# A batch-by-batch attention and bilinear FFN kernel: early batches one K chunk per head pair, first k and v over two fp32 queues, outputs at each strip's end, late loads behind the transposes of q

## The chip, the cores and the metric

The kernel runs on one core of a Trainium2 chip. Its metric is the device time of one execution in microseconds (us); lower is better. A core has TensorE (PE, matrix products into PSUM), VectorE (DVE), ScalarE (ACT), GpSimd (POOL) and SyncE (SP). Each engine takes its instructions in program order. Transfers are issued by SP, ACT or POOL; here POOL issues all that convert fp32 to bf16 on the way.

## The reference

```python
def _attn_ref(q, k, v, g_norm):            # q, k, v: 8 batches, 8 heads, 576 tokens, 64
    kv = np.einsum('bhsd,bhse->bhde', k, v)
    out = np.einsum('bhsd,bhde->bhse', q, kv)
    rms = np.sqrt(np.mean(out * out, axis=-1, keepdims=True) + 1e-06)
    return out / rms * g_norm
...
    x = attn_out.transpose(0, 2, 1, 3).reshape(B * S, H * D)      # 4608 tokens, 512
...
    a = x @ w_a                                                   # 512 to 1536
    b = x @ w_b
    return (a * b) @ w_out                                        # 1536 to 512
```

All inputs and the output are fp32. There is no softmax: for each head the kernel forms the 64x64 product of k and v, and multiplies q by it.

## The kernel before, in words

The work on TensorE is in bf16. The normalised x is kept transposed in four tiles `xt[0..3]`, 128 of the 512 model columns each (a "K chunk"), 4608 tokens long. The FFN goes over 9 strips of 512 tokens. For each strip there are 12 "units" (`Unit`, `ffn_ab`), one for each 128 of the 1536 inner columns: four matmuls with w_a, four with w_b (L205), a copy of the first product by ScalarE (L219) and a product by VectorE into `abt` (L221). Then come four output groups (`ffn_o`, `o_mm` L249, `o_out`), each 12 matmuls of 512 columns for 128 tokens, a copy to `o_sb` by VectorE and ScalarE in turn (L264, L262), and a store from SP (`store`, L242).

Attention goes batch by batch; batch b has 576 tokens, so strip s needs batches up to s, and strip s + 1 needs batch s + 1. For a batch: `kv` (L131) multiplies k by v for each pair of heads, `kv_out` (L140) copies that to bf16, `x` (L164, L171) multiplies q by it and squares the result, and `ss` (L176, L179, L184) sums the squares over a head with a matmul, takes the reciprocal root on ScalarE, and writes `xt` on VectorE.

q must be there transposed (`qT`, two tiles in turn). Batches 0 and 1 (`EARLY`) load q with tokens on partitions and transpose on TensorE (`qtr`, L147). For batches 2 to 7, `load_late` loads k and v, and copies q to a DRAM tile `qs` in bf16; then `transpose_q` (L118) has SP issue one transposing transfer from qs to qT. k and v have three buffers (`NB`), so load_late(b) waits for kv of batch b - 3.

Heads p and p + 4 make a pair, so that one x group of two pairs fills chunks m and m + 2; the chunks are used in the order `KORD`.

The program's order is written out by hand. POOL's queue: the pairs of batch 0, w_a and w_b in pieces of 256 columns (`load_ab`), w_out in 12 pieces (`load_o`), the pairs of batch 1, then `load_late` of batches 2 to 7. TensorE: dummy matmuls on zeros between the pieces of batch 0 (L310 to L328), strip 0's units, strip 0's outputs interleaved with batch 1 (L341 to L367), and then from strip 1 on a loop (L395) that sets pieces of the batch b = s + 1 between the units (`slices`), and the outputs of the strip before behind every third unit. transpose_q and load_late of the batch after the next are issued behind unit 6 of a strip. PSUM has 8 banks: units rotate through banks 0 to 2, outputs have bank 3 (`O`), x has banks 4 and 5 (early also 0 and 1), the sums 6 and 7, kv a part of 6 or 7.

Of the kernel before, what the change touches and what calls it, by code (L numbers as in the profile page):

```python
# [15 lines left out]
def kernel(  # L16
# [23 lines left out]
    EPS = 1e-6  # L40

    EC, EP = 6, 96
    EARLY = 2

    KORD = (0, 2, 1, 3)

    pool = ctx.enter_context(tc.tile_pool(name="sb", bufs=1))
    psum = ctx.enter_context(tc.tile_pool(name="ps", bufs=1, space=bass.MemoryType.PSUM))
# [26 lines left out]
    zeros = sb([128, 128], BF16, "zeros")  # L75
    g_col = sb([128, 1], FP32, "g_col")
    eps_t = sb([128, 1], FP32, "eps_t")
    warm = sb([128, 1], FP32, "warm")
    xv = [xt_i for xt_i in xt]

    P = psum.tile([128, 8, STRIP], FP32, name="P", tag="P")
    O = 3
# [6 lines left out]
    def load_heads(b, t, src, hs):  # L89
        nc.gpsimd.dma_start(  # L90
            out=t[:, hs, :, :], in_=src[b, hs].rearrange("h (t c) d -> t h c d", c=EC)
        )

    def load_pair(b, p):
        hs = slice(p, H, NP)
        load_heads(b, kt[b % NB], k, hs)
        load_heads(b, vt[b % NB], v, hs)
        load_heads(b, qt[b], q, hs)
# [6 lines left out]
        nc.gpsimd.dma_start(out=wo_t[:, i, :], in_=wo_v[:, i, :])  # L105

    def load_late(b):
        load_heads(b, kt[b % NB], k, slice(0, H))
        load_heads(b, vt[b % NB], v, slice(0, H))
        d = qs_d[b].rearrange("t (p j d) -> t p j d", p=NP, j=2)  # L110
        for j in range(2):
            nc.gpsimd.dma_start(  # L112
                out=d[:, :, j, :],
                in_=q[b, j * NP : (j + 1) * NP].rearrange("h t d -> t h d"),
            )

    def transpose_q(b):
        nc.sync.dma_start_transpose(qT[b % 2], qs_d[b])  # L118


    class Attn:
        def __init__(self, b):
            self.b = b
            self.kvs = kvs[b % 2]
            self.qT = qT[b % 2]

        def kv(self, p, o):

            for c in range(EC):
                for j in range(2):  # L130
                    nc.tensor.matmul(  # L131
                        o[j * D : (j + 1) * D, :],
                        lhsT=kt[self.b % NB][:, p + j * NP, c, :],
                        rhs=vt[self.b % NB][:, p + j * NP, c, :],
                        start=(c == 0),
                        stop=(c == EC - 1),
                    )
# [4 lines left out]
        def qtr(self, p, i0, i1):
            for h, i in ((0, i0), (1, i1)):
                t = P[:, i, :].bitcast(BF16)[:, 0:HF].rearrange("q (c t) -> q c t", c=EC // 2)
                for c in range(EC // 2):
                    for j in range(2):
                        nc.tensor.transpose(  # L147
                            t[j * D : (j + 1) * D, c, :],
                            qt[self.b][:, p + j * NP, h * (EC // 2) + c, :],
                            ident[0:EP, 0:EP],  # L150
                        )
                dst = self.qT[:, p, h * HF : (h + 1) * HF]
                src = P[:, i, :].bitcast(BF16)[:, 0:HF]
                if h:
                    nc.scalar.copy(dst, src)
                else:
                    nc.vector.tensor_copy(dst, src)
# [36 lines left out]
    class Unit:  # L194
# [15 lines left out]
                    stop=(kc == KORD[-1]),  # L210
                )

        def first(self):
            self.mm(wa_t, KORD[:2])
            self.mm(wb_t, KORD[:2])

        def rest(self, kcs=KORD):
            self.mm(wa_t, kcs)
# [64 lines left out]
    make_identity(nc, ident)  # L283
# [26 lines left out]
    dummy(30, 0)  # L310
    kv1(A, 0)
    A.qtr(0, 2, 3)
    dummy(4, 0)
    kv1(A, 1)
    A.qtr(1, 2, 3)
    dummy(6, 0)
    A.x(0, 0, X0)
    A.x(0, 1, X1)
    kv1(A, 2)
    A.qtr(2, 2, 3)  # L320
    A.ss(0, 0, SS, X0)
    dummy(4, 2)
    A.ss(0, 1, SS, X1)
    kv1(A, 3)
    A.qtr(3, 2, 3)
    dummy(6, 2)
    A.x(1, 0, X0)
    A.x(1, 1, X1)  # L328
    u0 = Unit(0, 0, 2, 3)
    u1 = Unit(0, 1, 0, 1)  # L330
    u0.first()
    A.ss(1, 0, SS, X0)
    A.ss(1, 1, SS, X1)
    u0.rest(KORD[2:])
    u1.rest()
    n_ab[0] = 2
# [8 lines left out]
    A.qtr(0, 2, 1)
    o_mm(0, 1, O, h1)
    kv1(A, 1)
    A.qtr(1, 2, 1)
# [3 lines left out]
    A.qtr(2, 2, 1)
    A.x(0, 0, X0)
    o_mm(0, 2, O, h1)
    A.x(0, 1, X1)
    A.ss(0, 0, SS, X0)
# [15 lines left out]
    u0.first()
    A.ss(1, 1, SS, X1)
    u0.rest(KORD[2:])
    u1.rest()
    n_ab[0] = 2


    def slices(A, per):
        kb = P[:, 7, 0 : NP * D].rearrange("q (p e) -> q p e", e=D)  # L380
        for p in range(NP):
            A.kv(p, kb[:, p, :])
            if p % per == per - 1:
                if p == NP - 1:
                    A.kv_out(0, NP, kb)
                yield
        for i, (m, h) in enumerate(((0, 0), (1, 0), (0, 1), (1, 1))):
            A.x(m, h, X0)
            yield
            A.ss(m, h, SS, X0)  # L390
            yield
            if i < 3:
                yield

    for s in range(1, N_STRIP):  # L395
        b = s + 1
        gen = slices(Attn(b), 4 if s == 1 else 2) if b < B else iter(())
        for fc in range(FC):
            if s > 1 or fc > 1:
                ffn_ab(s, fc)  # L400
            if s > 1 or fc > 0:
                next(gen, None)
            if fc % 3 == 2 and s > 1:
                ffn_o(s - 1, fc // 3)
                next(gen, None)
            if fc == 6 and b + 1 < B:
                transpose_q(b + 1)
                if b + 2 < B:
                    load_late(b + 2)
        for _ in gen:  # L410
            pass
# [41 lines left out]
```

## Time and profile before

| | |
|---|---|
| median of 3 runs | 357.5 us (356.81 to 357.6) |
| the profiled execution: its time | 358.61 us |
| its span, first to last instruction | 356.8 us |
| mean granted TensorE clock | 0.955 |
| busy, TensorE / VectorE / ScalarE / POOL | 324.0 / 120.2 / 125.8 / 59.9 us |
| moved by transfers | 32.19 MB |

The profile is of one execution. Matmuls are pipelined, so that a row of four matmuls of 512 columns lasts 1.03 us though the next group can start before its end; the distance of starts is what a group costs. The granted clock is 1.00 at 2.4 GHz and 0.50 at 1.2 GHz. In the waits a line names who waited, for whose result, and how long.

### The profile page before, as it was taken

To read this page: it belongs to the slowest core of one execution; us is meant where nothing else is said; L and a number is where in the kernel's file an instruction comes from. 1 tells how busy PE (TensorE), PEld (TensorE's weight loads), DVE (VectorE), ACT (ScalarE), POOL (GpSimd) and SP (SyncE) were. 2 spreads that over 40 slices of the span, in tenths; PEclk is the share of its full clock that TensorE was granted. 3 is DMA by queue.
4 is the path that set the end of the run, shared out by engine and by line. 5 is a ranking of instruction groups with operands and counts; after the bars stand their busy time and mean duration, and the time that the engine had idled before them with its cause. 6 is when DMAs were issued, how large, how long until landed. Compare 5 with 4: busy or idle time off the path is not lost.

```text
span 356.8 us, 4969 instructions
## 1 busy us (share of the span) xinstructions
PE 324.0 (91%) x1996; PEld 152.0 (43%) x2030; DVE 120.2 (34%) x204; ACT 125.8 (35%) x214; POOL 59.9 (17%) x78
## 2 busy tenths in 40 slices
PE   5779998706979999999999999999999999999996
PEld 4524443302434444444444444444444444444443
DVE  0323422301452543344434434352435232332311
ACT  2433334402453444344334433542453312223201
POOL 8845985230005000500000000000000000000000
PEclk9569999975999999999999999999999999999999
DMA  7999999999913940694100400130001000010022
GB/s 97 188 196 201 199 211 209 194 148 148 177 14 46 184 96 29 99 160 113 43 26 20 112 31 29 48 79 31 29 31 29 30 32 29 29 59 32 29 59 90
DMA packets 70024, 32.19 MB, mean 90 GB/s; under 512 B 43760, under 2 KB 65520, under 8 KB 70000
## 3 DMA queue, kind: packets, MB, share of 16 engines
q0 software_dynamic: 50304, 18.88, 46.4%
q1 hardware_dynamic: 19696, 12.98, 14.4%
q8 instruction: 16, 0.26, 0.3%
q14 instruction: 8, 0.07, 0.1%
HBM read 37.75 MB, written 12.98 MB: 142 GB/s over the span
## 4 chain that ended last, share of the span: by engine, by line
PE 68%; issue 0%; ACT 0%; ACTq 0%
PE P L205 41%; PE P L249 23%; PE P L131 1%; PE P L164 1%; PE P L176 1%; ACT osb L262 0%; ACT osb L421 0%; ACTq L421 0%
## 5 line engine op out<-in xcount | busy, mean ns | idle before, releaser
L221 DVE TENSOR_TENSOR ab<-P,asb 128x512 bf16<-128x512 f32 x108 | 74.7, 692 | 154.0 <-PE P L205 150.2
L205 PE MATMUL P<-xt,wa_t 128*128 128x512 bf16 x422 | 113.9, 387 | 5.2 <-DVE xt L184 4.1
L205 PE MATMUL P<-xt,wb_t 128*128 128x512 bf16 x424 | 113.0, 385 | 0.5
L249 PE MATMUL P<-wo_t,ab 128*128 128x512 bf16 (+1 forms) x428 | 97.4, 373 | 1.6 <-ACT osb L262 0.7
L219 ACT CAST asb<-P 128x512 bf16<-128x512 f32 x108 | 63.3, 586 | 93.6 <-PE P L205 93.1
L205 PEld LDWEIGHTS <-wb_t 128*128 128x128 bf16 x432 | 42.9, 99 | 53.4 <-issue 4.2
L249 PEld LDWEIGHTS <-ab 128*128 128x128 bf16 x444 | 42.7, 98 | 48.7 <-issue 1.1
L205 PEld LDWEIGHTS <-wa_t 128*128 128x128 bf16 x432 | 40.4, 99 | 48.9 <-issue 7.5
L184 DVE SCALAR_TENSOR_TENSOR xt<-P,g_col,rs 128x288 bf16<-128x288 f32 x64 | 30.1, 513 | 23.5 <-ACT rs L179 23.5
L171 ACT ACTIVATE sq<-P 128x576 bf16<-128x576 f32 x32 | 20.6, 652 | 41.6 <-PE P L164 41.6
L179 ACT ACTIVATE rs<-P,eps_t 128x576 f32<-128x576 f32 x32 | 23.7, 741 | 25.7 <-PE P L176 25.7
L264 DVE COPY osb<-P 128x512 f32<-128x512 f32 x18 | 12.4, 691 | 38.9 <-PE P L249 33.7
L262 ACT COPY osb<-P 128x512 f32<-128x512 f32 x17 | 10.0, 586 | 41.9 <-PE P L249 27.9
L90 POOL DMA_DIRECT2D kt<-in_k_dram x14 | 11.0, 786 | 75.9 <-PE P L131 70.2
L164 PE MATMUL P<-qT,kvs 64*64 64x288 bf16 x128 | 10.4, 328 | 12.1 <-DMA qT<-qs 12.1
L112 POOL DMA_DIRECT2D qs<-in_q_dram x12 | 20.5, 2018 | 4.2 <-DMA qs<-in_q_dram 3.1
L176 PE MATMUL P<-sq,ones 128*128 128x288 bf16 x64 | 14.1, 305 | 2.6 <-ACT rs L179 1.6
L131 PE MATMUL P<-vt,kt 96*64 96x64 bf16 x384 | 10.1, 202 | 5.2 <-DMA vt<-in_v_dram 3.5
L164 PEld LDWEIGHTS <-kvs 64*64 64x64 bf16 x128 | 3.6, 108 | 23.9 <-issue 21.3
L131 PEld LDWEIGHTS <-kt 96*64 96x64 bf16 x384 | 8.3, 116 | 12.4 <-issue 11.4
L176 PEld LDWEIGHTS <-ones 128*128 128x128 bf16 x64 | 6.4, 103 | 10.5 <-issue 4.4
L90 POOL DMA_DIRECT2D vt<-in_v_dram x14 | 10.8, 768 | 0.2
(26 smaller groups left out, 52.5 us busy)
## 6 DMA issues: line engine op xcount, KB each, us to landing
out_dram<-osb SPq DMA_DIRECT2D x23, 256.0 KB, 2.0
kt<-in_k_dram POOLq DMA_DIRECT2D x6, 576.0 KB, 11.1
vt<-in_v_dram POOLq DMA_DIRECT2D x6, 576.0 KB, 13.8
qs<-in_q_dram POOLq DMA_DIRECT2D x12, 288.0 KB, 15.3
out_dram<-osb SPq DMA_DIRECT2D x14, 128.0 KB, 2.3
wa_t<-in_moe_w_a_dram POOLq DMA_DIRECT2D x6, 256.0 KB, 10.0
wb_t<-in_moe_w_b_dram POOLq DMA_DIRECT2D x6, 256.0 KB, 10.3
wo_t<-in_moe_w_out_dram POOLq DMA_DIRECT2D x12, 128.0 KB, 5.9
```

The costliest lines, as they stand in the source:

```text
L90: nc.gpsimd.dma_start(out=t[:, hs, :, :], in_=src[b, hs].rearrange("h (t c) d -> t h c d", c=EC))
L112: nc.gpsimd.dma_start(out=d[:, :, j, :], in_=q[b, j * NP : (j + 1) * NP].rearrange("h t d -> t h d"),)
L131: nc.tensor.matmul(o[j * D : (j + 1) * D, :], lhsT=kt[self.b % NB][:, p + j * NP, c, :], rhs=vt[self.b % NB][:, p + j * NP, c, :], start=( ...
L164: nc.tensor.matmul(P[c * D : (c + 1) * D, i0 + j, 0:HF], lhsT=self.kvs[r, 2 * m + c, :], rhs=self.qT[r, 2 * m + c, ts], start=True, stop=True,
L171: nc.scalar.activation(sq[(2 * m + h) % 3], P[:, i0 : i0 + 2, 0:HF], AF.Square)
L176: nc.tensor.matmul(P[:, i0 + j, 0:HF], lhsT=ones, rhs=sq[n][:, j, :], start=True, stop=True)
L179: nc.scalar.activation(rs[n], P[:, i0 : i0 + 2, 0:HF], AF.Abs_reciprocal_sqrt, bias=eps_t)
L184: nc.vector.scalar_tensor_tensor(out=xt[m + 2 * j][:, t0 : t0 + HF], in0=P[:, x0 + j, 0:HF], scalar=g_col, in1=rs[n][:, j, :], op0=ALU.mul ...
L205: nc.tensor.matmul(self.a if w is wa_t else self.b, lhsT=w[:, kc, self.fc * 128 : (self.fc + 1) * 128], rhs=xt[kc][:, t0 : t0 + STRIP], st ...
L219: nc.scalar.copy(self.t, self.a)
L221: nc.vector.tensor_mul(abt[self.s % 2][self.fc], self.b, self.t)
L249: nc.tensor.matmul(P[:, i, e0:e1], lhsT=abt[s % 2][fc][:, g * 128 : (g + 1) * 128], rhs=wo_t[:, fc, e0:e1], start=(fc == 0), stop=(fc == F ...
```

## The change

- Batches 0 and 1 take heads 2p and 2p + 1 as a pair (`load_pair`, `head`), so that pair p gives chunk p of x. `x` and `ss` are replaced for them by `px`, `psq`, `pss`, `pst`, one pair at a time; `qtr` transposes a whole pair into one bank, and VectorE alone copies it. `KORD` is 0, 1, 2, 3.
- k and v of batch 0's first pair come as fp32, k from SP and v from ScalarE's queue, and are cast by VectorE and ScalarE. POOL makes the identity before its first load.
- The dummy matmuls have 512 columns: 8 ahead, and 2 + 4 for each of the pairs 0 to 2.
- The first 256 columns of w_a and w_b come in two pieces each, by K chunks.
- Batch 1 is spread more finely between the outputs of strip 0.
- load_late has q before k and v. For b above 2 it begins with a copy of one element on POOL, which reads the qT tile that transpose_q(b - 1) writes.
- From strip 1 on a strip's four outputs follow its own 12 units, with two banks in turn; the pieces of the batch stand at fixed places (`slot`). transpose_q(3) and load_late(4) come behind strip 1; transpose_q(b + 1) and load_late(b + 2) behind unit 8 of the strips from 2 on. The last strip stands by itself.

```diff
-    KORD = (0, 2, 1, 3)
+    KORD = tuple(range(KC))
...
     def load_pair(b, p):
-        hs = slice(p, H, NP)
+        hs = slice(2 * p, 2 * p + 2)
...
     def load_late(b):
-        load_heads(b, kt[b % NB], k, slice(0, H))
-        load_heads(b, vt[b % NB], v, slice(0, H))
+        if b > EARLY:
+
+            nc.gpsimd.tensor_copy(gate, qT[(b - 1) % 2][0:1, 0, 0:1])
         d = qs_d[b].rearrange("t (p j d) -> t p j d", p=NP, j=2)
...
+        load_heads(b, kt[b % NB], k, slice(0, H))
+        load_heads(b, vt[b % NB], v, slice(0, H))
...
+        def qtr(self, p, i, parts=1):
+            t = P[:, i, :].bitcast(BF16)[:, 0:S].rearrange("q (c t) -> q c t", c=EC)
+            for c in range(EC):
+                for j in range(2):
+                    nc.tensor.transpose(
+                        t[j * D : (j + 1) * D, c, :],
+                        qt[self.b][:, self.head(p, j), c, :],
+                        ident[0:EP, 0:EP],
+                    )
+            n = S // parts
+            for i0 in range(0, S, n):
+                nc.vector.tensor_copy(
+                    self.qT[:, p, i0 : i0 + n], P[:, i, :].bitcast(BF16)[:, i0 : i0 + n]
+                )
+
+
+        def px(self, p, i0):
+            for h in range(2):
+                for j in range(2):
+                    r = slice(j * D, (j + 1) * D)
+                    nc.tensor.matmul(
+                        P[r, i0 + h, 0:HF],
+                        lhsT=self.kvs[r, p, :],
+                        rhs=self.qT[r, p, h * HF : (h + 1) * HF],
+                        start=True,
+                        stop=True,
+                    )
+
+        def psq(self, p, i0):
+            nc.scalar.activation(sq[p % 3], P[:, i0 : i0 + 2, 0:HF], AF.Square)
+
+        def pss(self, p, i0, hs=(0, 1)):
+            for h in hs:
+                nc.tensor.matmul(
+                    P[:, i0 + h, 0:HF], lhsT=ones, rhs=sq[p % 3][:, h, :], start=True, stop=True
+                )
+            h0, h1 = hs[0], hs[-1] + 1
+            nc.scalar.activation(
+                rs[p % 3][:, h0:h1, :],
+                P[:, i0 + h0 : i0 + h1, 0:HF],
+                AF.Abs_reciprocal_sqrt,
+                bias=eps_t,
+            )
+
+        def pst(self, p, x0, hs=(0, 1)):
+            for h in hs:
+                t0 = self.b * S + h * HF
+                nc.vector.scalar_tensor_tensor(
+                    out=xt[p][:, t0 : t0 + HF],
+                    in0=P[:, x0 + h, 0:HF],
+                    scalar=g_col,
+                    in1=rs[p % 3][:, h, :],
+                    op0=ALU.mult,
+                    op1=ALU.mult,
+                )
...
     g_src = g_norm.rearrange("(d u) -> d u", u=1)
+    make_identity(nc, ident)
+    nc.sync.dma_start(out=k32, in_=pair_src(k, 0))
+    nc.scalar.dma_start(out=v32, in_=pair_src(v, 0))
     nc.vector.memset(zeros, 0.0)
-    load_pair(0, 0)
+    load_heads(0, qt[0], q, slice(0, 2))
...
-    for i in range(d_ff // WC):
+    for c in range(0, KC, 2):
+        for w, src in ((wa_t, wa_v), (wb_t, wb_v)):
+            nc.gpsimd.dma_start(out=w[:, c : c + 2, 0:WC], in_=src[:, c : c + 2, 0:WC])
+    for i in range(1, d_ff // WC):
...
+    X, SS = (4, 0), 6
...
+    nc.vector.tensor_copy(kt[0][:, 0:2], k32)
+    nc.scalar.copy(vt[0][:, 0:2], v32)
+    dummy(8, 0)
+    for p in range(NP):
+        last = p == NP - 1
+        kv1(A, p)
+        if p:
+            A.pss(p - 1, SS)
+        A.qtr(p, 2 + p % 2, 2 if last else 1)
+        if last:
+            A.px(p, X[1])
+            nc.scalar.activation(sq[p % 3][:, 0, :], P[:, X[1], 0:HF], AF.Square)
+            A.pst(p - 1, X[0])
+            nc.scalar.activation(sq[p % 3][:, 1, :], P[:, X[1] + 1, 0:HF], AF.Square)
+        else:
+            if p:
+                A.pst(p - 1, X[(p - 1) % 2])
+            dummy(2, 7)
+            A.px(p, X[p % 2])
+            A.psq(p, X[p % 2])
+            dummy(4, 3)
     u0 = Unit(0, 0, 2, 3)
...
+    u1 = Unit(0, 1, 4, 5)
+    u0.first((0, 1))
+    A.pss(3, SS, (0,))
+    A.pst(3, X[1], (0,))
+    u0.first((2,))
+    A.pss(3, SS, (1,))
+    A.pst(3, X[1], (1,))
+    u1.first((0, 1, 2))
+    u0.rest((3,))
+    u1.rest((3,))
...
     ffn_o(0, 0)
+    o_mm(0, 1, O, h1)
     kv1(A, 0)
...
+    A.qtr(0, 2)
     o_mm(0, 1, O, h2)
     o_out(0, 1, O)
+    A.px(0, X[0])
+    A.psq(0, X[0])
+    kv1(A, 1)
+    A.qtr(1, 2)
+    A.pss(0, SS)
+    A.pst(0, X[0])
+    o_mm(0, 2, O, h1)
...
     transpose_q(2)
-    load_late(3)
     u0 = Unit(1, 0, 2, 3)
...
+    def slot(A, s, n):
+
         kb = P[:, 7, 0 : NP * D].rearrange("q (p e) -> q p e", e=D)
...
+        k0, kn, xs = (4, 1, (6, 9, 11, 13)) if s < 3 else (1, 2, (4, 7, 10, 12))
+        if k0 <= n < k0 + kn:
+            for p in range((n - k0) * NP // kn, (n - k0 + 1) * NP // kn):
+                A.kv(p, kb[:, p, :])
+            if n == k0 + kn - 1:
+                A.kv_out(0, NP, kb)
         for i, (m, h) in enumerate(((0, 0), (1, 0), (0, 1), (1, 1))):
...
+            if n == xs[i]:
+                A.x(m, h, X[0])
+            if n == xs[i] + 1:
+                A.ss(m, h, SS, X[0])
+
+    for s in range(1, N_STRIP - 1):
         b = s + 1
...
+        A = Attn(b) if b < B else None
+        for n in range(FC + 4):
+            if n >= FC:
+                i = O if n % 2 == 0 else n_ab[0] % 3
+                n_ab[0] += n % 2
+                ffn_o(s, n - FC, i)
+            elif s > 1 or n > 1:
+                ffn_ab(s, n)
+            if A:
+                slot(A, s, n)
+            if n == 8 and b + 1 < B:
+                if s > 1:
+                    transpose_q(b + 1)
+                    if b + 2 < B:
+                        load_late(b + 2)
+                else:
+                    load_late(3)
+        if s == 1:
+            transpose_q(3)
+            load_late(4)
     last = N_STRIP - 1
+    for fc in range(FC):
+        ffn_ab(last, fc)
```

## Rows read from the trace of the kernel before

**Rows 1.** The page, parts 1 and 2: engines; granted clock and transfers in 40 slices.
```profile
PE 324.0 (91%) x1996; PEld 152.0 (43%) x2030; DVE 120.2 (34%) x204; ACT 125.8 (35%) x214; POOL 59.9 (17%) x78
...
PEclk9569999975999999999999999999999999999999
...
GB/s 97 188 196 201 199 211 209 194 148 148 177 14 46 184 96 29 99 160 113 43 26 20 112 31 29 48 79 31 29 31 29 30 32 29 29 59 32 29 59 90
```

**Rows 2.** Windows: from:to length, then busy us and instructions; PEclk, DMA share, GB/s.
```profile
45.58:68.80 23.22, 19.44 (x184) 9.08 (x185) 7.39 (x16) 9.75 (x20) 12.80 (x10) 1.00 1.64 208
68.80:83.60 14.80, 2.70 (x56) 1.61 (x57) 1.38 (x2) 0.96 (x2) 4.78 (x4) 0.74 1.71 150
83.60:89.50 5.90, 5.89 (x18) 2.24 (x18) 1.25 (x3) 1.98 (x3) 0.00 (x0) 0.50 1.67 156
...
141.02:175.70 34.68, 34.47 (x212) 15.74 (x216) 13.46 (x22) 14.14 (x23) 4.80 (x4) 1.00 0.68 99
```

**Rows 3.** Waits of TensorE, 68 to 110 us: total, times, longest.
```profile
PE P L164 <- DMA qT<-qs: 12.1, 1, 12.1
PE P L205 <- DVE xt L184: 1.2, 1, 1.2
PE P L176 <- ACT sq L171: 0.8, 1, 0.8
```

**Rows 4.** Timeline, 62 to 100 us: start, length, engine, operation.
```profile
63.79 20.58 SPq L118 DMA_TRANSPOSE qT<-qs  x2
...
83.61 0.45 PE L164 MATMUL P<-qT,kvs 64*64 64x288 bf16 x4 [12.05 <-DMA qT<-qs]
```

**Rows 5.** The tile qT: time from a transfer's issue to its landing.
```profile
DMA to landing us min/median/max: 4.6/5.2/19.8
```

**Rows 6.** Timelines of TensorE, 4 to 29, and of all engines, 20 to 45 us.
```profile
5.85 0.38 PE L131 MATMUL P<-vt,kt 96*64 96x64 bf16 x12 [1.53 <-DMA vt<-in_v_dram]
...
9.42 0.54 PE L131 MATMUL P<-vt,kt 96*64 96x64 bf16 x12 [2.02 <-DMA vt<-in_v_dram]
...
28.32 1.03 PE L205 MATMUL P<-xt,wa_t 128*128 128x512 bf16 x4
...
29.18 1.03 PE L205 MATMUL P<-xt,wb_t 128*128 128x512 bf16 x4
```

**Rows 7.** Timeline of POOL, 0 to 30 and 40 to 250 us.
```profile
2.07 0.64 POOL L90 DMA_DIRECT2D vt<-in_v_dram  x1
2.70 0.63 POOL L90 DMA_DIRECT2D qt<-in_q_dram  x1
...
4.49 0.63 POOL L90 DMA_DIRECT2D vt<-in_v_dram  x1
...
59.94 3.25 POOL L112 DMA_DIRECT2D qs<-in_q_dram  x2
```

**Rows 8.** The page, part 6: transfers, KB each, us to landing.
```profile
out_dram<-osb SPq DMA_DIRECT2D x23, 256.0 KB, 2.0
```

**Rows 9.** Groups of instructions: busy us, mean ns; idle before.
```profile
L184 DVE SCALAR_TENSOR_TENSOR xt<-P,g_col,rs 128x288 bf16<-128x288 f32 x64 | 30.1, 513 | 23.5 <-ACT rs L179 23.5
L179 ACT ACTIVATE rs<-P,eps_t 128x576 f32<-128x576 f32 x32 | 23.7, 741 | 25.7 <-PE P L176 25.7
...
L264 DVE COPY osb<-P 128x512 f32<-128x512 f32 x18 | 12.4, 691 | 38.9 <-PE P L249 33.7 <-remote 5.3
```

**Rows 10.** Waits of TensorE, 44 to 70 us.
```profile
PE P L205 <- DVE xt L184: 1.4, 1, 1.4
PE P L131 <- ACT rs L179: 0.8, 1, 0.8
PE P L147 <- DVE xt L184: 0.6, 1, 0.6
PE P L176 <- ACT rs L179: 0.4, 1, 0.4
```

**Rows 11.** The tile qs: time from a transfer's issue to its landing.
```profile
DMA to landing us min/median/max: 4.6/11.6/30.6
```

More of the change, by code (lines that the diff above doesn't have):

```diff
@@ L74 @@
     ones = sb([128, 128], BF16, "ones")
-    zeros = sb([128, 128], BF16, "zeros")
+    zeros = sb([128, STRIP], BF16, "zeros")
     g_col = sb([128, 1], FP32, "g_col")
@@ L78 @@
     warm = sb([128, 1], FP32, "warm")
-    xv = [xt_i for xt_i in xt]
+    k32 = sb([EP, 2, EC, D], FP32, "k32")
+    v32 = sb([EP, 2, EC, D], FP32, "v32")
+    gate = sb([1, 1], BF16, "gate")
     P = psum.tile([128, 8, STRIP], FP32, name="P", tag="P")
@@ L125, in __init__, with head @@
             self.qT = qT[b % 2]
+        def head(self, p, j):
+            return 2 * p + j if self.b < EARLY else p + j * NP
         def kv(self, p, o):
@@ L132, in kv @@
                         o[j * D : (j + 1) * D, :],
-                        lhsT=kt[self.b % NB][:, p + j * NP, c, :],
-                        rhs=vt[self.b % NB][:, p + j * NP, c, :],
+                        lhsT=kt[self.b % NB][:, self.head(p, j), c, :],
+                        rhs=vt[self.b % NB][:, self.head(p, j), c, :],
                         start=(c == 0),
@@ L140, in kv_out @@
             nc.scalar.copy(self.kvs[:, p0:p1, :], src)
[L142 to L157, printed above, removed]
+        def qtr(self, p, i, parts=1):
[12 more added lines that the diff above has]
+                )
@@ L211, in mm, with first @@
                 )
-        def first(self):
-            self.mm(wa_t, KORD[:2])
-            self.mm(wb_t, KORD[:2])
+        def first(self, kcs):
+            self.mm(wa_t, kcs)
+            self.mm(wb_t, kcs)
         def rest(self, kcs=KORD):
@@ L269, in ffn_o, with dummy, pair_src @@
         o_out(s, g, i)
-    def dummy(n, i):
+    def dummy(n, i, cols=STRIP):
         for _ in range(n):
-            nc.tensor.matmul(P[:, i, 0:128], lhsT=zeros, rhs=zeros, start=True, stop=True)
+            nc.tensor.matmul(
+                P[:, i, 0:cols], lhsT=zeros[:, 0:128], rhs=zeros[:, 0:cols], start=True, stop=True
+            )
+    def pair_src(src, p):
+        return src[0, 2 * p : 2 * p + 2].rearrange("h (t c) d -> t h c d", c=EC)
     g_src = g_norm.rearrange("(d u) -> d u", u=1)
+    make_identity(nc, ident)
+    nc.sync.dma_start(out=k32, in_=pair_src(k, 0))
+    nc.scalar.dma_start(out=v32, in_=pair_src(v, 0))
     nc.vector.memset(zeros, 0.0)
-    load_pair(0, 0)
+    load_heads(0, qt[0], q, slice(0, 2))
     nc.sync.dma_start(out=g_col[0:D, :], in_=g_src)
@@ L282 @@
     nc.scalar.activation(warm, eps_t, AF.Abs_reciprocal_sqrt)
-    make_identity(nc, ident)
     nc.vector.memset(ones, 0.0)
@@ L304, in kv1 @@
         A.kv_out(p, p + 1, kslot(p))
-    X0, X1, SS = 4, 0, 6
+    X, SS = (4, 0), 6
     A = Attn(0)
[L310 to L328, printed above, removed]
-    u0 = Unit(0, 0, 2, 3)
[L330 to L336, printed above, removed]
+    nc.vector.tensor_copy(kt[0][:, 0:2], k32)
[19 more added lines that the diff above has]
+            dummy(4, 3)
+    u0 = Unit(0, 0, 2, 3)
+    u1 = Unit(0, 1, 4, 5)
[8 more added lines that the diff above has]
+    u1.rest((3,))
     for fc in range(2, FC):
@@ L343 @@
     ffn_o(0, 0)
+    o_mm(0, 1, O, h1)
     kv1(A, 0)
[L345 to L348, printed above, removed]
+    A.qtr(0, 2)
     o_mm(0, 1, O, h2)
     o_out(0, 1, O)
-    kv1(A, 2)
[L352 to L356, printed above, removed]
+    A.px(0, X[0])
[5 more added lines that the diff above has]
+    o_mm(0, 2, O, h1)
+    A.px(1, X[1])
+    A.psq(1, X[1])
+    kv1(A, 2)
+    A.qtr(2, 2)
@@ L357 @@
+    A.pss(1, SS)
+    A.pst(1, X[1])
     o_mm(0, 2, O, h2)
     o_out(0, 2, O)
-    A.ss(0, 1, SS, X1)
+    A.px(2, X[0])
+    A.psq(2, X[0])
     kv1(A, 3)
-    A.qtr(3, 2, 1)
+    A.qtr(3, 2)
+    A.pss(2, SS)
+    A.pst(2, X[0])
     o_mm(0, 3, O, h1)
-    A.x(1, 0, X0)
+    A.px(3, X[1])
+    A.psq(3, X[1])
     o_mm(0, 3, O, h2)
     o_out(0, 3, O)
-    A.x(1, 1, X1)
-    A.ss(1, 0, SS, X0)
+    A.pss(3, SS)
+    A.pst(3, X[1])
     transpose_q(2)
-    load_late(3)
     u0 = Unit(1, 0, 2, 3)
-    u1 = Unit(1, 1, 0, 1)
@@ L372 @@
[L372 to L379, printed above, removed]
-        kb = P[:, 7, 0 : NP * D].rearrange("q (p e) -> q p e", e=D)
[L381 to L386, printed above, removed]
-        for i, (m, h) in enumerate(((0, 0), (1, 0), (0, 1), (1, 1))):
[L388 to L393, printed above, removed]
@@ L395 @@
-    for s in range(1, N_STRIP):
-        b = s + 1
[L397 to L411, printed above, removed]
+    u1 = Unit(1, 1, 4, 5)
@@ new lines @@
+    u0.first((0, 1, 2))
+    u1.first((0, 1, 2))
+    u0.rest((3,))
+    u1.rest((3,))
+    n_ab[0] = 0
+    def slot(A, s, n):
+        kb = P[:, 7, 0 : NP * D].rearrange("q (p e) -> q p e", e=D)
+        k0, kn, xs = (4, 1, (6, 9, 11, 13)) if s < 3 else (1, 2, (4, 7, 10, 12))
[4 more added lines that the diff above has]
+                A.kv_out(0, NP, kb)
+        for i, (m, h) in enumerate(((0, 0), (1, 0), (0, 1), (1, 1))):
+            if n == xs[i]:
+                A.x(m, h, X[0])
+            if n == xs[i] + 1:
+                A.ss(m, h, SS, X[0])
```

## The prediction

> **What bounds the kernel now.** I read the page first. TensorE is busy 324.0 of 356.8 us, the other engines 35% or less [rows 1]: what neither shortens TensorE's row nor fills a hole in it is worth nothing. The clock's row shows where holes are: half speed in the second slice, little more in the third, low again in slices 9 and 10 (one slice is 8.9 us), full speed otherwise [rows 1]. The transfers' row stands near 200 GB/s from the second slice to the eighth, then falls [rows 1].
>
> The windows put sizes on this. A strip in the steady part takes 34.68 us with 34.47 busy [rows 2]: nothing is to be won there unless matmuls are removed, and none are. So the change is worth what it does before about 107 us. Two stretches are bad there. From 68.8 to 83.6 only 2.70 us are busy [rows 2], and the waits name the cause: 12.1 us for the transfer of qT from qs [rows 3]. The timeline shows that SP issued this transpose at 63.79 and that the first matmul on it ran at 83.61 [rows 4]. A transpose lands in 4.6 us at best, 5.2 at the median, 19.8 at worst [rows 5]; this one is the worst. In those 20 us the loads of later batches share the transfer engines with it, since load_late waits only for its buffers: POOL issues the q of batch 4 at 59.94 [rows 7]. The second bad stretch is the start: the second unit of strip 0 gives way to the third only at 28.32 us [rows 6].
>
> **The change part by part**, against the profiled execution's 358.6 us (span 356.8 and 1.8 around it).
>
> *The late loads and the transpose of batch 2.* load_late(3) now begins with a POOL copy that reads what transpose_q(2) wrote; only later late loads queue behind it on POOL. So this transpose runs against nothing newer than batch 2. What must have landed before: three batches at 3 x 590 KB (bf16) and 4.72 MB of weights, 10.0 MB; at 200 GB/s [rows 1] that is 50 us after a start near 3, and the outputs of strip 0 (1.05 MB) share the engines, so about 56. SP issues the transpose behind the last store of strip 0, some 1.7 us behind that output's last matmul (0.7 for the copy [rows 9], 1 for hand-over and the stores, an estimate), by the sum below near 59.4. It may meet a tail of v; I take 5.2 to 8 us. The first x of batch 2 also moves, from behind unit 2 to behind unit 6 of strip 1. With units at 1.73 us (two groups of four, starts 0.86 apart [rows 6]) and 1.0 for kv (four groups like that at 5.85, without their tails [rows 6]) it comes 9.6 us after unit 1, which by the sum ends at 61.4: at 71.0, 11.6 after the issue. The wait of 12.1 goes, and nothing takes its place if the transpose keeps under 11.6.
>
> With the wait goes the slow clock behind it: 5.90 us at a granted 0.50, full of work [rows 2]; at full clock half of it, 2.9. At the end of strip 1 the last x and sums ran with nothing beside them, at 0.8 and 1.2 us of waiting [rows 3]; now outputs of 2.6 us each (12 x 0.215) stand there. Together 12.1 + 2.9 + 2.0 = **17.0 less**; with a transpose as slow as 19.8, 8.2 us of wait and the slow clock come back: 5.9 less.
>
> *The start.* Before, v of pair 0 is POOL's second load (2.07), q its third (2.70) [rows 7]; kv began at 5.85, when v was there, and kv of pair 1 at 9.42 [rows 6], when its v, issued at 4.49 [rows 7], was there. After, POOL makes the identity first (about 0.5: what lies between the end of q's issue at 3.33 and k's, one 0.63 ahead of 4.49 [rows 7]) and then has only q of pair 0, near 1.9, about v's old place, so each load of pair 1 leaves about 1.25 earlier (two issues of 0.63 [rows 7]): kv(1) can start at 8.2. The new fp32 loads with their casts have no row. Nearest below: stores of 256 KB issued by SP land in 2.0 us [rows 8]; above: v's 3.8 from POOL. A cast of 768 columns: by VectorE's 691 ns for 512 [rows 9], 1.04 at most; nothing at the least. So kt and vt stand between 3 and 6; either way q (near 5.7, 3.8 after its issue) and its transposes end pair 0 near 7.0. In SP's queue the g_col loads now stand behind k, in ScalarE's the warm-up behind v, each for one issue; their users come after 8 us.
>
> Then a chain for each pair: kv 0.38 [rows 6], its copy (about 0.3, an estimate below the 0.74 of a larger one [rows 9]), the sums 0.24 (two times 288 columns at the pace of [rows 6]), 0.17 until they are out (a group lasts 1.03 where its slot is 0.86 [rows 6]), the root 0.74 [rows 9], two dummies 0.43 (they write a bank which that root reads), px 0.25, four dummies 0.86: 3.4, with hand-overs 3.5. kv(3) comes at 8.2 + 2 x 3.5 = 15.2, px(3) ends near 17.5, and the 16 matmuls of units 0 and 1 are mixed with the last two half sums (root 0.74 or less, xt 0.51 [rows 9]): done near 21.5, against 28.32. I take **6.0 less** of the 6.8, for hand-overs missed. At best the chain is 2.9 a pair: 8.6 less. At worst the clock stays at half speed; then the 26 dummies of 512 columns cost 0.43 each, the chain 5.1, and units 0 and 1 end near 29.8: 1.5 more. Weights cover either case: each two units need 0.52 MB, 2.6 us at 200 GB/s, and take 3.46 on TensorE; the two load issues more that the first 256 columns cost lie on POOL alone.
>
> The Trainium skill has a rule that speaks against the cast on VectorE (SBUF — State Buffer, "SBUF: two separate sides"): while VectorE copies fp32 within SBUF in a mode that uses two ports, POOL cannot write the descriptors of its own loads, and these come late. By that rule the loads of pair 1 would lose up to that cast, at most 1.04 us by the bound above, and the sum would read 1.0 more; no row of before has such a copy, so the sum stays.
>
> *Batch 1 between the outputs of strip 0.* This stretch lasts 23.2 us with 19.44 busy [rows 2]; its dependency waits are 1.4 + 0.8 + 0.6 + 0.4 = 3.2 [rows 10], and the finer order, with other work between root and use, covers them. It makes new ones: the second output follows the first in the same bank, and waits for VectorE's 0.69 [rows 9] and 0.2; three sums come about 0.3 too early for the square and the kv copy that ScalarE does before them. 3.2 - 1.8: **1.4 less**; bounds 3.2 less and 0.8 more.
>
> *Outputs at each strip's end, two banks in turn.* The same 144 matmuls a strip, so nothing by itself. In strips 1 and 2 an x stands only one unit behind the sums (n = 10, 11): root and two xt products take 0.17 + 0.74 + 2 x 0.51 = 1.9 plus hand-overs, against 1.73 of matmuls: 0.35 each, **0.7 more** (0 to 2).
>
> Sum: 358.6 - 17.0 - 6.0 - 1.4 + 0.7 = 334.9 for a profiled execution. The median of the runs stands 1.1 below the profiled one (357.5 against 358.6): **333.8 us**.
>
> **Rivals.** *The start stays at half clock.* For: before, with short bursts between waits for loads, the clock's row reads 0.9 in the first slice and 0.5 in the second [rows 1]. Against: there are now some 2.5 us of matmuls in each 3.5. Then the start costs 1.5 more instead of 6.0 less: 341.3.
>
> *The transpose is late anyway: the gate does not do what it is there for.* It does not hold batch 2's own k and v, and if these run much longer than 56 us the transpose shares with them as it did with others: 8.2 us of wait and 2.9 of clock, 344.9. Against: 11.6 us of room, and q now goes ahead of k and v.
>
> *Slower: a chain of gates.* transpose_q(3) stands behind strip 1's stores, load_late(4) waits for it, transpose_q(4) on SP waits for that load, and x of batch 4 waits for that in strip 3 (n = 4): 34.7 + 5 x 1.73 + 1.0 - 1 = 43 us after the first issue. At the medians it takes 5.2 [rows 5] + 3.3 (POOL's two issues of q [rows 7]) + 11.6 (the landing of qs [rows 11]) + 5.2 = 25; with each at its worst 19.8 + 3.3 + 30.6 [rows 5, 7, 11] + 19.8 = 73, which makes 30 us of idle and 3 of clock: 367. From a chain of about 64 on the change loses. Against: those worst values arose with many loads at once, which the gate forbids.
>
> **How the numbers follow.** Forecast 0.66, its own range 329 to 338.5 (all three gains at their best; half of the start's gain and the new waits at their worst); cold start 0.17; late transpose 0.09; chain of gates 0.04, nearly all of it slower; sizes outside all this 0.04. The range that leaves out no more than 2 in 10 runs from 329 to 341.5. About 0.2% can be told from no change here. Faster 0.95, within it 0.01, slower 0.04.
>
> **What would show it.** Right: TensorE waits for no qT, and the clock's row has no fall after the start; the transpose of batch 2 lands within 8 us, with no load of batch 3 issued before; kv of pairs 1 to 3 stand about 3.5 apart; unit 2 of strip 0 starts near 22, strip 1's third unit near 61; strips keep 34.7. Wrong: a granted 0.50 between 8 and 20 us, a wait on qT anywhere, a transpose on SP with stores queued behind it while TensorE idles, or first casts that end after 7.

## The result and the profile after

The changed kernel took 335.66 us (median of 4 runs, 333.26 to 337.11); the kernel before beside it 357.31. The ratio is 0.9389, with an interval of 0.9328 to 0.945. The forecast was 333.8 us in a range of 329.0 to 341.5. One execution each of three versions below, 379.53 to 556.08 us at a mean granted clock of 0.56 to 0.86, is left out of the ranges given, and moves no median by more than 0.5 us. Of the profiled execution (334.78 us, span 333.0) the page's parts 1 and 2 read, to be set beside [rows 1]:

```profile
PE 320.4 (96%) x1971; PEld 148.1 (44%) x2006; DVE 122.3 (37%) x206; ACT 123.5 (37%) x209; POOL 60.8 (18%) x83
...
PEclk9999999999999999999999999999999999999999
...
GB/s 139 197 196 199 200 194 214 105 100 115 65 108 82 177 104 214 145 127 119 103 72 164 52 98 94 0 0 86 43 0 2 63 63 3 0 94 33 1 31 94
```

TensorE is busy for almost the same time as before, 320.4 against 324.0 us; 24 us of span have gone. So holes were closed, and little work was saved. The transfers' row shows how: what had stood near 200 GB/s in one block up to 71 us is now cut after the seventh slice and spread over the strips. The longest waits of TensorE over the whole span (us in total, times, longest):

```profile
PE P L183 <- ACT kvs L148: 1.9, 6, 0.4
PE P L139 <- ACT vt L368: 1.3, 1, 1.3
PE P L321 <- DVE eps_t L336: 1.2, 1, 1.2
PE P L321 <- ACT rs L187: 0.9, 2, 0.5
PE P L296 <- DVE osb L311: 0.8, 1, 0.8
PE P L154 <- DMA qt<-in_q_dram: 0.5, 1, 0.5
PE P L170 <- DVE qT L161: 0.4, 1, 0.4
```

No line waits for qT from qs, which stood first in [rows 3] with 12.1 us. On SP's and POOL's timelines the gate can be followed: the transposes of batches 2, and 3 and 4 in one row; the POOL copies that wait for those of batches 2 and 4; and the landing times of the tile qT (against [rows 4, 5]):

```profile
60.89 2.19 SPq L123 DMA_TRANSPOSE qT<-qs  x1
...
96.06 21.21 SPq L123 DMA_TRANSPOSE qT<-qs  x2
```

```profile
66.06 0.18 POOL L112 COPY gate<-qT 1x1 bf16<-1x1 bf16 x1 [19.02 <-DMA qT<-qs]
...
119.40 0.18 POOL L112 COPY gate<-qT 1x1 bf16<-1x1 bf16 x1 [12.63 <-DMA qT<-qs]
```

```profile
DMA to landing us min/median/max: 4.8/5.9/9.8
```

The transpose of batch 2 was issued at 60.89 and had landed by 66.06, 5.2 us later; the first x on it ran at 72.5. The chain of gates, the slower rival, took 119.4 - 96.06 = 23.3 us from the issue of batch 3's transpose to the landing of batch 4's (the forecast had 25 by the medians, and 43 allowed). The windows of the stretches (columns as in [rows 2]; batch 1 between the outputs, then strips 1 and 3):

```profile
41.71:62.81 21.10, 19.20 (x182) 9.40 (x184) 7.50 (x15) 7.51 (x15) 5.03 (x5) 1.00 1.24 179
62.81:97.00 34.19, 33.87 (x212) 15.68 (x215) 14.05 (x23) 14.29 (x25) 4.94 (x5) 1.00 0.69 97
...
131.70:166.40 34.70, 34.49 (x214) 15.74 (x216) 13.45 (x22) 14.07 (x24) 4.94 (x5) 1.00 0.88 127
```

The second row holds a strip from its third unit to the next strip's first two; it has no hole; before, the 14.80 us with 2.70 busy of [rows 2] stood at its head. TensorE's timeline of the start, against [rows 6]:

```profile
6.14 0.53 PE L139 MATMUL P<-vt,kt 96*64 96x64 bf16 x12 [1.34 <-ACT vt L368]
...
9.40 1.53 PE L321 MATMUL P<-zeros 128*128 128x512 bf16 x4
10.86 0.38 PE L139 MATMUL P<-vt,kt 96*64 96x64 bf16 x12
...
13.66 1.04 PE L321 MATMUL P<-zeros 128*128 128x512 bf16 x4
14.63 0.38 PE L139 MATMUL P<-vt,kt 96*64 96x64 bf16 x12
...
18.40 0.38 PE L139 MATMUL P<-vt,kt 96*64 96x64 bf16 x12
...
24.44 1.03 PE L252 MATMUL P<-xt,wa_t 128*128 128x512 bf16 x4
```

Every kv of batch 0 comes later than before, the last one at 18.40 instead of 16.24, yet unit 2 starts at 24.44 instead of 28.32. Behind the last kv, TensorE waited before for a root and for xt, and its matmuls stood at half pace:

```profile
16.24 0.53 PE L131 MATMUL P<-vt,kt 96*64 96x64 bf16 x12 [0.83 <-ACT rs L179]
...
21.98 0.41 PE L176 MATMUL P<-sq,ones 128*128 128x288 bf16 x2 [0.83 <-ACT rs L179]
23.83 0.80 PE L205 MATMUL P<-xt,wa_t 128*128 128x512 bf16 x2 [1.44 <-DVE xt L184]
...
25.18 1.91 PE L205 MATMUL P<-xt,wa_t 128*128 128x512 bf16 x4
```

In the changed kernel the longest wait there is 0.40 us. The four dummies at 9.40 take 1.46 us until the next kv, those at 13.66 only 0.97: up to about 10 us the matmuls run at half pace, though the clock's row reads 9 there (90% or more).

### The profile page after: what moved, and what is told of

The parts are those of the page before. It is cut to its first block, busy times and chain, and to the rows that moved or that the text cites. A ratio compares the mean times of both kernels' runs of the same rounds, so it can differ in the third digit from the quotient of the medians.

```text
span 333.0 us, 4922 instructions
## 1 busy us (share of the span) xinstructions
PE 320.4 (96%) x1971; PEld 148.1 (44%) x2006; DVE 122.3 (37%) x206; ACT 123.5 (37%) x209; POOL 60.8 (18%) x83
## 3 DMA queue, kind: packets, MB, share of 16 engines
q1 hardware_dynamic: 19904, 13.28, 15.3%
## 4 chain that ended last, share of the span: by engine, by line
PE 94%; DMA 2%; ACT 2%; issue 1%; DVE 0%; POOL 0%; POOLq 0%
PE P L252 56%; PE P L296 28%; PE P L139 2%; PE P L211 2%; PE P L223 2%; DMA qt<-in_q_dram 2%; PE P L321 2%; PE P L170 1%; PE P L183 1%; ACT sq L179 1%; ACT rs L187 0%; PE P L154 0%; ACT kvs L148 0%; DVE osb L311 0%; ACT osb L309 0%
## 5 line engine op out<-in xcount | busy, mean ns | idle before, releaser
L252 PE MATMUL P<-xt,wb_t 128*128 128x512 bf16 x431 | 111.6, 379 | 0.4
L252 PE MATMUL P<-xt,wa_t 128*128 128x512 bf16 x409 | 109.6, 380 | 1.0 <-issue 0.2
L226 ACT ACTIVATE rs<-P,eps_t 128x576 f32<-128x576 f32 x24 | 17.8, 742 | 16.6 <-PE P L223 16.6
L218 ACT ACTIVATE sq<-P 128x576 bf16<-128x576 f32 x24 | 15.6, 652 | 18.3 <-PE P L211 18.3
L112 POOL COPY gate<-qT 1x1 bf16<-1x1 bf16 x5 | 0.9, 178 | 103.1 <-DMA qT<-qs 103.1
L115 POOL DMA_DIRECT2D qs<-in_q_dram x12 | 19.3, 1821 | 1.9 <-issue 1.8
L92 POOL DMA_DIRECT2D kt<-in_k_dram x13 | 14.8, 1141 | 0.6 <-DMA vt<-in_v_dram 0.4
L92 POOL DMA_DIRECT2D vt<-in_v_dram x13 | 14.8, 1135 | 0.9 <-DMA qt<-in_q_dram 0.8
L321 PE MATMUL P<-zeros 128*128 128x512 bf16 x25 | 9.2, 503 | 2.1 <-DVE eps_t L336 1.2
L223 PE MATMUL P<-sq,ones 128*128 128x288 bf16 x48 | 9.8, 286 | 0.0
```

What stands on the lines that cost most here:

```text
L92: nc.gpsimd.dma_start(out=t[:, hs, :, :], in_=src[b, hs].rearrange("h (t c) d -> t h c d", c=EC))
L115: nc.gpsimd.dma_start(out=d[:, :, j, :], in_=q[b, j * NP : (j + 1) * NP].rearrange("h t d -> t h d"),)
L218: nc.scalar.activation(sq[(2 * m + h) % 3], P[:, i0 : i0 + 2, 0:HF], AF.Square)
L223: nc.tensor.matmul(P[:, i0 + j, 0:HF], lhsT=ones, rhs=sq[n][:, j, :], start=True, stop=True)
L226: nc.scalar.activation(rs[n], P[:, i0 : i0 + 2, 0:HF], AF.Abs_reciprocal_sqrt, bias=eps_t)
L252: nc.tensor.matmul(self.a if w is wa_t else self.b, lhsT=w[:, kc, self.fc * 128 : (self.fc + 1) * 128], rhs=xt[kc][:, t0 : t0 + STRIP], st ...
```

## The experiments

**Is it the gate that removed the wait, or the later place of the first x?** Three variants of the changed kernel make a table of both with it. First the gate alone, on the kernel before:

```diff
+    gate = sb([1, 1], BF16, "gate")
...
     def load_late(b):
+        if b > EARLY:
+            nc.gpsimd.tensor_copy(gate, qT[(b - 1) % 2][0:1, 0, 0:1])
```

> The kernel before with nothing but the gate. If the gate removes the wait, the transpose of batch 2 lands about 5 us after its issue near 63.8, ahead of the first x at 71.5: no wait on qT, no slow clock behind it, 342 to 343 us (15 less). Rival: the wait only moves, to the transpose of batch 3, whose load now starts later, or the transpose is slow whatever else is in flight: 350 us or more.

Measured: 344.89 us (343.99 to 345.33) against 355.89 (353.35 to 357.16) of the kernel before on the same chip, ratio 0.9691 (0.9642 to 0.9741). No wait on qT is left; all landings of this kernel's qT:

```profile
DMA to landing us min/median/max: 4.6/4.9/6.5
```

The medians differ by 11.0 us where 15 had been expected. The profiles bear out the 15: from behind strip 1's second unit to the end they differ by 14.9 us (356.8 - 68.8 against 342.7 - 69.6). But the profiled execution of the kernel before, 358.61 us from an earlier set of runs, is among the slowest of this kernel (349.61 to 358.7), so 11.0 is the better measure of what the gate gives it. The wait did not move elsewhere. This version still loads k and v ahead of q, so the gate needs no new order of the loads. Next the changed kernel without the gate:

```diff
     def load_late(b):
-        if b > EARLY:
-            nc.gpsimd.tensor_copy(gate, qT[(b - 1) % 2][0:1, 0, 0:1])
```

> The changed kernel without the POOL copy that holds the late loads back; everything else as changed. If the gate removes the wait of 12.1 us, the transpose of batch 2 lands near 20 us after its issue again, TensorE waits 6 to 9 us for qT in strip 1 and then runs some 3 us more at half clock: 345 to 347 us. Rival: moving the first x behind unit 6, and q ahead of k and v, is enough; then no wait on qT and 335 to 337 us.

Measured: 338.77 us (337.71 to 339.82), ratio 0.9528 (0.9483 to 0.9572). Neither expectation fits. The transpose was slower again, but TensorE waited little; its wait, the tile's landings, and the start of unit 2 of strip 0:

```profile
PE P L208 <- DMA qT<-qs: 1.0, 1, 1.0
```

```profile
DMA to landing us min/median/max: 4.5/5.1/12.7
```

```profile
26.28 1.03 PE L249 MATMUL P<-xt,wa_t 128*128 128x512 bf16 x4
```

The profiled execution (337.71 us) is 2.9 us slower than that of the changed kernel; 1.0 of it is the wait, and 1.8 lies in the start (26.28 against 24.44). So the later place alone hides most of a transpose of 12.7 us, but not all: no execution of this version was faster than 337.71 us, and none of the changed kernel slower than 337.28. The other three executions, up to 339.82, were not profiled. To see both at work, the x of strip 1 went three units ahead, once without the gate and once with it:

```diff
         k0, kn, xs = (4, 1, (6, 9, 11, 13)) if s < 3 else (1, 2, (4, 7, 10, 12))
+        if s == 1:
+            k0, xs = 2, (3, 6, 9, 12)
```

> The changed kernel without the gate, and in strip 1 with kv behind unit 2 and the first x behind unit 3, so three units ahead of the changed place. Without the gate the transpose landed 12.7 us after its issue and TensorE waited 1.0 us. If gate and later place each stand in for the other, the wait comes back as 5 to 7 us, with up to 3 us of slow clock: 342 to 348 us. Rival: the gate is idle in this kernel, the transpose is quick whenever it is issued: 337 to 339 us.

> The same early x with the gate in place. The transpose landed near 66.1 us and the x is wanted near 67.2: no wait, 333 to 337 us like the changed kernel. Rival: the later place was what removed the wait, and it comes back: 338 us or more.

Measured: 346.83 us (344.64 to 347.66) without the gate, 334.9 (334.71 to 335.36) with it. TensorE's timeline without the gate:

```profile
77.80 0.45 PE L208 MATMUL P<-qT,kvs 64*64 64x288 bf16 x4 [6.89 <-DMA qT<-qs]
78.19 1.89 PE L249 MATMUL P<-xt,wa_t 128*128 128x512 bf16 x4
79.87 1.91 PE L249 MATMUL P<-xt,wb_t 128*128 128x512 bf16 x4
```

The wait is back with 6.89 us, the transpose took 13.4, and behind it groups of four matmuls stand 1.68 apart instead of 0.86 [rows 6]. With neither gate nor later place the medians differ by 11.9 us; the two profiles differ by 12.3, of which 2.8 lie before strip 1's third unit (66.31 against 63.53) and 9.5 are the wait and the slow clock. The gate alone removes the wait, the place alone all but 1.0 us of it. With the gate the early x ran at 68.07, only 0.4 us behind the landing. All three variants load q ahead of k and v, which by itself does not make the transpose quick.

**What is the start made of?** The loads first: k and v of pair 0 by POOL, no fp32 buffers, no casts.

```diff
...
-    nc.sync.dma_start(out=k32, in_=pair_src(k, 0))
-    nc.scalar.dma_start(out=v32, in_=pair_src(v, 0))
...
-    load_heads(0, qt[0], q, slice(0, 2))
+    load_pair(0, 0)
...
-    nc.vector.tensor_copy(kt[0][:, 0:2], k32)
-    nc.scalar.copy(vt[0][:, 0:2], v32)
```

> The changed kernel with k and v of the first pair loaded by POOL in bf16, without the fp32 buffers and casts. The trace of the changed kernel shows the first kv at 6.14 us, behind the cast of v, against 5.85 before, so the two fp32 queues seem to win nothing for pair 0. If they matter only through POOL's queue, pairs 1 to 3 land 1.3 us later; TensorE's chain of pairs hides that, and the time stays within 1 us of the changed kernel's 335.7. Rival, the forecast's reason: the start hangs on when the loads arrive; then 337 us.

Measured: 334.86 us (334.69 to 336.06), ratio 0.9425 (0.9384 to 0.9466): no gain from the two fp32 queues shows, though the changed kernel was not timed beside it. kv(0) ran at 5.69 and kv(1) at 10.85 us, as against 6.14 and 10.86. q of pair 0 was there at the same time: issued at 2.85 it took 4.2 us, against 1.49 and 5.7 beside the fp32 loads. Then the dummies in the loop over the pairs:

```diff
-            dummy(2, 7)
...
-            dummy(4, 3)
```

> The changed kernel without the 2 + 4 dummy matmuls in the loop over pairs 0 to 2. If these keep the clock up, the clock stays at half speed through the start and units 0 and 1 of strip 0 run at half pace: 337 to 340 us. Rival: they only lengthen the chain of each pair, by 1.3 us at full clock; without them units begin up to 4 us earlier and the time falls to 332 us.

Measured: 334.81 us (334.59 to 334.82), ratio 0.9414 (0.9368 to 0.946): both theories miss. The timeline shows them cancel:

```profile
8.83 0.52 PE L139 MATMUL P<-vt,kt 96*64 96x64 bf16 x12
...
12.09 0.53 PE L139 MATMUL P<-vt,kt 96*64 96x64 bf16 x12
...
15.43 0.53 PE L139 MATMUL P<-vt,kt 96*64 96x64 bf16 x12
...
18.63 1.03 PE L252 MATMUL P<-xt,wa_t 128*128 128x512 bf16 x2
...
24.24 1.03 PE L252 MATMUL P<-xt,wa_t 128*128 128x512 bf16 x4
```

The chain is shorter (3.3 us a pair), but at half clock (kv 0.53), and the units that follow run at half pace for longer: unit 2 starts at 24.24, against 24.44. The same kernel as changed, run again beside the next three versions:

> The changed kernel itself, once more beside its variants. Its four times went from 333.3 to 337.1 us. If this spread comes from the point at which TensorE's clock rises in the start (matmuls of the dummies 0.43 us apart until about 10 us in its profile), a profile with another time shows that point moved, and all else equal: 333 to 337 us. Rival: the spread comes from transfers, and later stretches differ.

Measured: 334.6 us (332.82 to 337.28, 6 runs), ratio 0.9365 (0.9326 to 0.9405). The profile is of the run that took 337.28:

```profile
9.59 1.89 PE L321 MATMUL P<-zeros 128*128 128x512 bf16 x4
...
15.28 1.89 PE L321 MATMUL P<-zeros 128*128 128x512 bf16 x4
...
19.90 1.04 PE L321 MATMUL P<-zeros 128*128 128x512 bf16 x4
...
26.91 1.03 PE L252 MATMUL P<-xt,wa_t 128*128 128x512 bf16 x4
```

Half pace lasts until about 17 us here, and unit 2 starts at 26.91: 2.47 later than in the run of 334.78, which is the whole difference of 2.5 us. To take away the hole ahead of the first kv:

```diff
-    dummy(8, 0)
+    dummy(12, 0)
```

> The changed kernel with 12 dummy matmuls ahead of the first kv instead of 8, so that TensorE has no hole between 4.8 us and the cast of v at 6.1. If the clock in the start sets the time, it is up from pair 0 on: 1 to 2 us less than the changed kernel on the same chip, and times closer together. Rival: pair 0 waits for the cast and the q load, the clock falls in those holes anyway: no difference within 0.5 us.

Measured: 333.47 us, ratio 0.9331 (0.9301 to 0.9362), and all five runs between 333.05 and 334.03. Its timeline runs at full pace from the first kv on:

```profile
6.09 0.38 PE L139 MATMUL P<-vt,kt 96*64 96x64 bf16 x12
...
9.55 0.38 PE L139 MATMUL P<-vt,kt 96*64 96x64 bf16 x12
...
23.13 1.03 PE L252 MATMUL P<-xt,wa_t 128*128 128x512 bf16 x4
```

The spread falls from 4.5 us in the run above, on the same chip, to 1.0. The median falls by 1.1, with intervals that overlap, and the lowest time (333.05 against 332.82) not at all: what is gone is the slow starts. Then the order of a pair's pieces, with two dummies fewer and the others in other banks:

```diff
         kv1(A, p)
+        A.qtr(p, 2 + p % 2, 2 if last else 1)
         if p:
             A.pss(p - 1, SS)
-        A.qtr(p, 2 + p % 2, 2 if last else 1)
...
-            dummy(2, 7)
+            dummy(2, 2 + (p + 1) % 2)
...
-            dummy(4, 3)
+            dummy(2, 2 + (p + 1) % 2)
```

> The changed kernel with the pieces of a pair in another order: kv, transposes, sums of the pair before, two dummies in a bank that no root reads, x, two dummies. If the chain of a pair (3.77 us apart in the trace) is what sets the start, it falls to 2.2 to 2.6 us and unit 2 of strip 0 starts 3 to 4 us earlier: 331 to 332 us. Rival, the forecast's: with fewer dummies the clock stays at half speed, or the loads bind; 335 us or more.

Measured: 331.2 us (330.89 to 331.96), ratio 0.927 (0.924 to 0.9301). Order, number and banks are not told apart, and the chain of this version by itself is not shown; the next one has the same order. Both together:

> Both changes of the start together: 12 dummies ahead of the first kv, and the pieces of a pair in the new order with 2 + 2 dummies. If clock and chain are separate causes, it is faster than either alone (333.5 and 331.2 us): about 330 us. Rival: with the shorter chain the loads of pairs 1 to 3 bind, TensorE waits for them, and the 12 dummies win nothing more: 331 us.

Measured: 330.06 us (329.94 to 330.48). The chain of a pair is 2.35 to 2.6 us, and unit 2 starts at 19.66:

```profile
9.11 0.38 PE L139 MATMUL P<-vt,kt 96*64 96x64 bf16 x12
...
11.70 0.38 PE L139 MATMUL P<-vt,kt 96*64 96x64 bf16 x12
...
14.05 0.38 PE L139 MATMUL P<-vt,kt 96*64 96x64 bf16 x12
...
19.66 1.03 PE L252 MATMUL P<-xt,wa_t 128*128 128x512 bf16 x4
```

**Do the new waits of batch 1 cost anything?**

```diff
-    ffn_o(0, 0)
+    ffn_o(0, 0, n_ab[0] % 3)
+    n_ab[0] += 1
...
+    o_mm(0, 2, O, h1)
     A.pss(0, SS)
     A.pst(0, X[0])
-    o_mm(0, 2, O, h1)
```

(and the sums of pairs 1 and 2 likewise behind the half output that follows them)

> The changed kernel with strip 0's first output in a bank of its own, and the sums of batch 1 behind half an output instead of right behind the transposes. The forecast put 1.8 us of new waits there, and the trace shows 0.78 + 0.40 + 0.28 + 0.28: if they are on the path, 1.6 to 1.8 us less than the changed kernel on the same chip. Rival: the time comes back in the waits that follow (xt for strip 1's first units): no difference.

Measured: 335.05 us, ratio 0.9398 (0.9359 to 0.9437): the rival. The waits from 40 to 66 us are others, and as long:

```profile
PE P L296 <- DVE osb L311: 0.9, 1, 0.9
PE P L139 <- ACT rs L187: 0.9, 2, 0.5
```

The kv of the next pair writes into the bank whose root is now late, and an output copy stands behind two xt products on VectorE; the stretch takes 21.11 us, as against 21.10. So the last version gives kv another bank instead of another place (the diff is against the version with both changes of the start):

```diff
-        c = 288 + 64 * (p % 2)
-        return P[:, 6, c : c + 64]
+        return P[:, X[p % 2], 288:352]
...
-    ffn_o(0, 0)
+    ffn_o(0, 0, n_ab[0] % 3)
+    n_ab[0] += 1
```

> The version with both changes of the start, and besides the products of k and v of the early batches in the bank that their x takes next, so that no sum waits for their copy and no kv for a root, and the first output of strip 0 in a bank of its own. If the waits of 0.3 (six) and 0.78 us are on the path and are not given back, 1.5 to 2.5 us less than that version, near 328.5 us. Rival: they come back behind, as in the run with the other order of batch 1: no difference.

Measured: 328.87 us (328.35 to 329.49), on the same chip as the version with both changes of the start (330.06): 1.2 less. It is the fastest version of all, 5.7 us below the changed kernel's 334.6, though the two were not timed beside each other; the changed kernel with the early x took 334.9 on this chip. The gain is in batch 1: that stretch takes 19.85 us (37.44 to 57.29) instead of 21.11. The start gave 0.5 back in the profile (unit 2 at 20.17), since units 0 and 1 now wait for weights:

```profile
PE P L252 <- DMA wa_t<-in_moe_w_a_dram: 0.7, 1, 0.7
```

## Why the prediction was right

**The transpose of batch 2: right in cause, and in size against the profile; one thing understated.** Foreseen were a landing in 5.2 to 8 us, no wait, no slow clock and no hole at the end of strip 1: 17.0 less. Measured 5.2 us and none of the three, and behind strip 1's second unit the profiles differ by 17.8 us (356.8 - 68.8 against 333.0 - 62.8). The cause is shown by the gate alone (wait gone) and by the early x without it (6.9 us and the slow clock back). The forecast put the price of losing the gate at 11 us, from the 19.8 us of [rows 5]; without it the transpose took 12.7 and 13.4 in this kernel, so at the changed place TensorE waited 1.0 us, and the median, not timed beside it, stood 3.1 higher. That place is a second cover, which the forecast named but did not price by itself. The Trainium skill (DMA: Bandwidth & Descriptors, "Queues, rings and completion order") says that each transfer engine goes round between the queues that have work; the landings with and without company, 12.7 and 5.2 us, fit this, but no run tests how the engines share.

**The start: right in sign, too large.** 6.0 less was taken, 3.9 came (28.32 to 24.44). The step that failed is "kv(1) can start at 8.2": it ran at 10.86. What held it was no load of pair 1, for without loop dummies it ran at 8.83 and waited for none, but TensorE's own pair 0. The forecast let pair 0 end with its transposes near 7.0; its copy, x and six dummies, which stand ahead of kv(1) in program order (7.81 to 10.86), have no term there. q landed 5.7 us after its issue, not 3.8, so its earlier issue won nothing. The dummies ran at half pace: with 12 ahead, and full pace from the first kv, kv(1) ran at 9.55 and unit 2 at 23.13, so of the 2.1 us that are missing about 1.3 are the clock's. The chain was 3.77 us for 3.5. The forecast held two cases apart, full clock or half clock; the runs lie between them, by when the clock rises. That this sets the spread of the times is shown by the two profiles of the same kernel and by the 12 dummies. The fp32 loads landed at 5.05 and 5.25, sooner than POOL's v before (5.85), but their casts took 0.71 and 0.83 us, so kt and vt stood no sooner; rows of VectorE's and ScalarE's casts and of POOL's issues at that time:

```profile
4.74 0.64 POOL L92 DMA_DIRECT2D vt<-in_v_dram  x1
5.05 0.71 DVE L367 CAST kt<-k 96x768 bf16<-96x768 f32 x1 [3.48 <-DMA k<-in_k_dram]
5.25 0.83 ACT L368 CAST vt<-v 96x768 bf16<-96x768 f32 x1 [2.57 <-DMA v<-in_v_dram]
5.36 0.64 POOL L92 DMA_DIRECT2D qt<-in_q_dram  x1
```

POOL's issues beside the cast last 0.64 us like the others: the loss that the Trainium skill's rule (SBUF — State Buffer, "SBUF: two separate sides") would have brought is not seen in them. Pair 1's loads, for which the forecast feared it, had all been issued by 4.13, ahead of the cast. They landed 5.6 to 5.9 us after their issue, against 4.4 to 5.0 in the run with all loads on POOL; whether the fp32 loads beside them or the casts did that is not shown, and TensorE waited for none of pair 1's.

**Batch 1: right.** 1.4 less was taken, 2.1 came (23.22 to 21.10 us). The new waits were put at 1.8 and are 0.8 + 1.0 by the waits of that stretch; the old ones and some hand-overs went.

**Outputs at the strip's end: the 0.7 more did not come.** The x behind unit 11 of strip 2 lasts 0.47 instead of 0.32 us, no more, and strips keep 34.7. The end gained what the forecast left out: with strip 7's outputs done earlier, TensorE no longer waits 0.7 us for an output copy there.

Summed with what the profiles show: 358.6 - 3.9 - 2.1 - 17.8, of which 0.7 at the end, = 334.8, against 334.78 measured. The start came out 2.1 worse and three small terms 2.1 better, so the close agreement of the total is partly luck. The last step of the forecast, 1.1 less from the profiled execution to the median, failed: the median, 335.66, lies 0.9 above it, which the spread of the start allows (332.8 to 337.3). Of the rivals, the cold start was half true, the late transpose and the chain of gates did not occur. Where the start's 3.9 us come from can be read roughly from three profiles. From the last kv to unit 2 it was 12.1 us before (16.24 to 28.32), 8.8 in the run without loop dummies (15.43 to 24.24, half pace up to about 22), and 6.0 in the changed kernel (18.40 to 24.44). So some 3.3 us come from units 0 and 1 mixed with the half sums, at half pace in both, and 2.8 from the clock; 2.2 are lost by the later last kv. No run took the mixing away by itself.

## What to carry to other kernels

A transfer that the engine on the critical path waits for was made quick here by keeping later transfers out of its way: a one-element copy that reads its result, ahead of the later loads on their own queue, did it, and the same copy alone gave 11 us to the kernel before, where the whole change gave 22. Before a wait is removed by a new order, ask which bank or engine the moved work meets next; here one reordering gave its 1.8 us back at once, while other banks for the same work kept 1.2. When a kernel's times spread by more than one per cent, compare the starts of two profiles before trusting a small difference; here 2.47 of 2.5 us lay there.

## What was not expected of the hardware

- The granted clock reads 1.00 in each of the first five windows of 5 us of the changed kernel, while its dummies stand at half pace until 10 us in one profile and 17 us in another. The distance of equal matmuls is the surer reading there.
- Loads of 295 KB in fp32, k from SP and v from ScalarE's queue, were usable 4.3 and 4.5 us after their issue (0.75 to 5.05, 0.74 to 5.25). POOL's converting load of as many values took 3.8 us in the kernel before (2.07 to 5.85 [rows 6, 7]); q, issued by POOL beside the fp32 loads, took 5.7.
- The transposing transfer landed 4.6 to 5.6 us after its issue in the kernel before from strip 2 on, and 15.3 and 19.8 us in strip 1, beside loads of later batches; in the changed kernel without the gate 12.7 and 13.4. The gate moves some of this: batches 4 and 5, whose own k and v are issued 5 to 8 us ahead of their transposes, took 8.1 and 9.8 with it, which TensorE did not wait for.
